# Second mask product of the first quad moved to GpSimd, and transposes, loads and copies moved around it

## The chip, the cores and the metric

The kernel runs on one core of a Trainium2 chip. The metric is the device time of one launch in microseconds (us), as the median of several runs. A profile is one execution of the same program with the hardware profiler on. The engines are called by the profile's names: PE is TensorE (PEld its weight loads), DVE is VectorE, ACT is ScalarE, POOL is GpSimd, and SP is the engine whose queue issues the stores. Every engine runs its own instructions in the order in which they are written, and waits for semaphores of the others.

## The reference, cut to what matters

```python
# 8 batches, 8 heads, 512 local and 32 global tokens, head size 64
k_all, v_all = concat(k_g, k_l), concat(v_g, v_l)            # along the tokens
out_g = softmax(q_g @ k_all.T / 8) @ v_all                   # global tokens see everything
s_ll  = where(abs(i - j) <= 32, q_l @ k_l.T / 8, -1e9)       # local tokens see a band ...
s_lg  = q_l @ k_g.T / 8                                      # ... and the global tokens
out_l = softmax(concat(s_lg, s_ll)) @ concat(v_g, v_l)
x   = concat(out_g, out_l), heads side by side               # 4352 tokens x 512
h   = x @ w_in                                               # 512 -> 2048
out = (h * sigmoid(1.702 * h)) @ w_out                       # 2048 -> 512
```

The inputs and the output are float32; the kernel computes in bf16 with float32 accumulation.

## The kernel before

Work goes by batches. A batch's attention is done by two quads of four heads, objects of class `Wide`, each with its transposed keys `kT`, queries `qt` and `qc` (a packed copy of some query columns), and its exponentials `E[0]` and `E[1]`. The steps of a quad are methods. `Tk` and `Tq` transpose keys and queries on DVE (32x32 blocks), `kcopy`, `qcopy` and `ext` copy columns of them and of the global tokens into place, `S(rnd)` multiplies queries and keys for one of two rounds, `X(rnd)` takes exp on ACT (PSUM to SBUF), `M(rnd)` multiplies the result by a 0/1 mask in place, with both inputs in SBUF. `U(unit)` makes the row sums (unit 0) and the two halves of the output, `Gm` the output of the global queries into the bank `og`; `UG` is all four. `R` transposes and inverts the row sums, `XL(h)` normalizes an output half into `xL`, the input of the hidden product. `G` normalizes the global queries' output from `og` in PSUM: reciprocal, product, transpose into `xG`.

The two products of the feed-forward part are partly written with seven products instead of eight. `Pair` (second product, two per batch) and `HPair` (a part of the hidden product) have `mm(k)` for the seven, and `m3`, `z`, `zm`, `sub`, `evict`, `add` for the sums of their results, on DVE but for the ACT copies `m3` and `evict`. In an `HPair`, `mm(5)`, `mm(2)` and `mm(7)` accumulate onto PSUM halves that `m3`, `z` and `zm` have read before. `x_sums` makes four sums of halves of `xL` that `HPair` multiplies: three of 128x512 (L673) and a fourth of 128x1024 (L674), bf16, both inputs in SBUF; `mm(3)` and `mm(4)` read the second and third, `mm(6)` the fourth. `g_sums` does the same for the activations `gT` and `Pair`.

The steady part alternates two stages, with the order of each engine written out by hand:

- `h_some(i)`, i from 3 to 7, is the hidden product of batch i with its activations, and prepares the two quads that come next: `c`, the second quad of batch i+1, and `a2`, the first of batch i+2.
- `phase_o(i)`, i from 2 to 6, is the second product of batch i (`p0`, `p1`), interleaved with attention: `a` finishes (`UG`, `R`, `XL`, `G`), `c` goes from `S` to `G`, and `a2` goes through `S`, `X`, `M` of both rounds.

PSUM has four banks for products (`pbank`, in rotation) and two pairs of banks for scores (`spair`). In the next `h_some` the hidden matmuls of step 4 take the bank `px` of `p1`, once `sub` and `evict` have read it, and those of step 5 take `py`, once `add` has. `evict` is written before the ACT table load for the activation (`gelu_table`), `m3` of the `HPair` behind it.

POOL issues the loads: `load` brings the q and k of a batch (its buffers are used by every other batch), `load_v` the v of a batch in five chunks, each with the global rows behind it but for chunk 2. `vtiles` has two buffers, so batch i+3 takes the one of batch i+1. In `phase_o(i)` POOL does `a2.M(0)` and behind it `loads_after(i + 1)`, which is `load_v(i + 3)` and `load(i + 4)` as far as there are such batches: v in `phase_o` 2, 3 and 4, q and k in 2 and 3. In `h_some(i)` POOL does the copies of `c` and `a2`.

Of the kernel before, what the change touches and what calls it, by code (L numbers as in the profile page):

```python
# [12 lines left out]
F32 = mybir.dt.float32  # L13
BF16 = mybir.dt.bfloat16
# [6 lines left out]
def kernel(  # L21
# [12 lines left out]
    nc = tc.nc  # L34

    B, H, Sl, D = q_l.shape
# [23 lines left out]
    att = ctx.enter_context(tc.tile_pool(name="att", bufs=2))  # L60
# [14 lines left out]
    def load(b, us=(0, 1), kq=True):  # L75
        if b not in loaded:
            loaded[b] = (ld.tile([128, 2, 16 * D], BF16, name="rk"),
                         ld.tile([128, 2, 16 * D], BF16, name="rq"))
        if kq:
            s = slice(us[0], us[-1] + 1)  # L80
            nc.gpsimd.dma_start(out=loaded[b][1][:, s], in_=qf[b][:, s])
            nc.gpsimd.dma_start(out=loaded[b][0][:, s], in_=kf[b][:, s])
# [5 lines left out]
    def v_view(b, n):  # L88
        return vtiles[b % 2][:, : 8 * n * (D + 2)].rearrange("p (u j c d) -> p u j c d", u=2, j=4, c=n)

    def load_v(b, hs=slice(0, 8)):
        if b == 2:
            nc.gpsimd.memset(v_view(b, 5)[:, :, :, :, D:], 1.0)
        vt = v_view(b, 5).rearrange("p u j c d -> p (u j) c d")
        vs, vg = (x[b].rearrange("h s d -> s h d") for x in (v_l, v_g))
        for c in range(5):
            n = 128 if c == 2 else 96
            nc.gpsimd.dma_start(out=vt[0:n, hs, c, :D], in_=vs[FIRST[c] : FIRST[c] + n, hs])  # L98
            if c != 2 and b != 1:
                nc.gpsimd.dma_start(out=vt[96:128, :, c, :D], in_=vg)  # L100
# [11 lines left out]
    def on_act(out_, in_):  # L112
        nc.scalar.activation(out_, in_, AF.Copy)  # L113
# [11 lines left out]
    def load_g(lo, hi, names="kq"):  # L125
        for name, dst, src in (("k", rkg, kgf), ("q", rqg, qgf)):
            if name in names:
                nc.gpsimd.dma_start(out=dst[:, lo:hi, :], in_=src[:, lo:hi, :])
# [111 lines left out]
    def transpose_g(lo, hi, names="qk"):  # L240
        for name, dst, s in (("q", qgT, rqg), ("k", kgT, rkg)):
            if name not in names:
                continue
            nc.vector.transpose(dst[:, lo:hi, :32], s[:, lo:hi].bitcast(F32))
# [31 lines left out]
    xG_by_row = xG.rearrange("p k (a s f) -> p k a s f", a=2, f=4)  # L276
# [7 lines left out]
    def spair():  # L284
        return [psS.tile([128, 2, 512], F32, name="s4", tag="s%d" % i) for i in range(2)]
# [214 lines left out]
    class Wide(Quad):  # L500
# [100 lines left out]
        def UG(self):  # L601
            for unit in range(3):
                self.U(unit)
            self.Gm()

    gTs, ops = {}, {}
    HT = TB // 2
    HM = d_model // 2
# [26 lines left out]
    def exp_table():  # L635
        nc.scalar.activation(spot[:, 0:1], spot[:, 1:2], AF.Exp)
# [27 lines left out]
    def x_sums(i):  # L664
        t = xL[i]
        x11, x12, x21, x22 = (t[:, 2 * k : 2 * k + 2, h * HT : h * HT + HT] for k in range(2) for h in range(2))
        r1 = att.tile([128, 16, 32], F32, name="sT", bufs=1).rearrange("p a b -> p (a b)").bitcast(BF16)
        r2 = att.tile([128, 512], F32, name="rs", bufs=1).bitcast(BF16)
        xs["d"] = [r.rearrange("p (k t) -> p k t", k=2) for r in (
            r1[:, : 2 * HT], r1[:, 2 * HT :], moe.tile([128, 2 * HT], BF16, name="xs"))]  # L670
        xs["s"] = r2.rearrange("p (k t) -> p k t", k=NKC)
        for o, x, y, op in zip(xs["d"], (x11, x12, x21), (x22, x22, x11), (ALU.add, ALU.subtract, ALU.subtract)):
            nc.vector.tensor_tensor(o, x, y, op)  # L673
        nc.vector.tensor_tensor(xs["s"], t[:, :, :HT], t[:, :, HT:], ALU.add)  # L674
        xs["r"] = (x11, x22)
# [173 lines left out]
    a, c = Quad(0), Quad(1)  # L849
# [93 lines left out]
    a, c = nq[1]  # L943
# [71 lines left out]
    a, c = nq[2]  # L1015
# [22 lines left out]
    def loads_after(i):  # L1038
        if i + 2 < B:
            load_v(i + 2)  # L1040
        if i == 1:
            load_g(8, NQ)
        if i + 3 < B:
            load(i + 3)

    def quads_of(n):
        if n < B and n not in nq:
            nq[n] = (Wide(2 * n), Wide(2 * n + 1))
        return nq.get(n, (None, None))
# [44 lines left out]
    def phase_o(i):  # L1094
        b = i + 1
        a, c = nq[b]
        a2, c2 = quads_of(b + 1)
        p0, p1 = Pair(i, 0), Pair(i, 1)
        exp_table()
        a.UG()  # L1100
        c.S(0)
        a.R()
        g_sums(i, 7, 8, (0,))
        a.XL(0)
        g_sums(i, 7, 8, (1, 2))
        a.XL(1)
        g_sums(i, 7, 8, (3,))
        p0.mm(3, 4, 1)
        c.X(0)
        p0.m3()  # L1110
        p0.z()
        a.G()
        c.M(0)
        c.S(1)
        c.X(1)
        p0.mm(6)
        p0.zm()
        c.M(1)
        p0.mm(5, 2)
        p0.sub()  # L1120
        p0.evict()
        p0.mm(7)
        p0.add()
        p0.store()
        if a2:
            c.UG()
            c.R()
            a2.S(0)
            a2.X(0)
            a2.M(0, nc.gpsimd)  # L1130
            loads_after(i + 1)
        else:
            pt = spair()
            c.U(0, bank(pt, 0))
            c.U(1, bank(pt, 2))
            c.U(2, bank(pt, 3))
            c.Gm(bank(pt, 1))
            c.R()
        c.XL(0)
        if a2:  # L1140
            c.XL(1)
            c.G()
        p1.mm(3, 4)
        p1.m3()
        p1.z()
        if not a2:
            c.XL(1)
            c.G()
        p1.mm(1, 6)
        p1.zm()  # L1150
        x_sums(i + 1)
        if a2:
            a2.S(1)
            a2.X(1)
        p1.mm(5, 2)
        p1.sub()
        p1.evict()
        gelu_table()
        p1.mm(7)
        p1.add()  # L1160
        if a2:
            a2.M(1)
        p1.store()

    def h_some(i):
        c = nq[i + 1][1] if i + 1 < B else None
        a2 = quads_of(i + 2)[0] if i + 2 < B else None
        pool = nc.gpsimd.tensor_copy
        gTs[i] = moe.tile([128, FC, TB], BF16, name="gT")
        hps = [pbank("hp"), pbank("hp")]  # L1170
        for fc in range(2):
            h_mm(i, fc, hps[fc], range(NKC))
        p = HPair(i, 1)
        p.mm(3, 4)
        p.m3()
        for fc in range(2):
            h_act(i, fc, hps[fc])
        if c:
            c.Tk(False)
            c.kcopy(pool)  # L1180
        p.z()
        p.mm(1, 6)
        p.zm()
        if c:
            c.Tq(False)
            c.qcopy(pool)
            c.ext((3,), pool)
        if a2:
            a2.Tk(False)
            a2.kcopy(pool)  # L1190
        h_step(i, 4)
        if c:
            c.ext((0,), on_act)
        h_step(i, 5)
        p.mm(5, 2)
        p.sub()
        p.inner()
        p.mm(7)
        p.add()
        h_step(i, 6)  # L1200
        p.outer()
        if a2:
            a2.Tq(False)
            transpose_g(2 * i + 4, 2 * i + 6)
            a2.qcopy(pool)
            a2.ext(copy=pool)
        if c:
            g_sums(i, 0, 2)
        h_step(i, 7)
        if c:  # L1210
            c.ext((1,), on_act)
            g_sums(i, 2, 4)
            for fc in range(8, 12):
                h_step(i, fc)
                if fc == 9:
                    c.ext((2,), on_act)
            g_sums(i, 4, 6)
            h_step(i, 12)
            h_step(i, 13)
            g_sums(i, 6, 7)  # L1220
            h_step(i, 14)
            h_step(i, 15)
            return
        p = HPair(i, 4)
        p.mm(3, 4)
        p.m3()
        g_sums(i, 0, 2, (0, 1))
        p.z()
        p.mm(1, 6)
        p.zm()  # L1230
        g_sums(i, 0, 2, (2,))
        h_step(i, 10)
        h_step(i, 11)
        p.mm(5, 2)
        p.sub()
        p.inner()
        p.mm(7)
        p.add()
        g_sums(i, 0, 2, (3,))
        h_step(i, 12)  # L1240
        p.outer()
        for k in range(3):
            for lo in (2, 4):
                g_sums(i, lo, lo + 2, (k,))
        h_step(i, 13)
        h_step(i, 14)
        h_step(i, 15)
        g_sums(i, 6, 8, (0, 1, 2))
        g_sums(i, 2, 4, (3,))
        g_sums(i, 4, 6, (3,))  # L1250
        g_sums(i, 6, 8, (3,))

    for i in range(1, B):
        if i > 2:
            h_some(i)
        elif i > 1:
            for fc in range(FC):
# [3 lines left out]
                if i + 1 < B:  # L1261
                    c = nq[i + 1][1]
# [6 lines left out]
                    if fc == 9 and i + 2 < B:  # L1269
                        a2 = quads_of(i + 2)[0]  # L1270
# [19 lines left out]
    for st in range(FC):  # L1290
        h_step(B, st)
        if st < len(todo):
            tt, k = todo[st]
            if k == 3:
                p = Pair(B - 1, tt, pair_banks(tt))
# [19 lines left out]
    p = Pair(B, 0, (x0, x1, y0, y1))  # L1315
# [53 lines left out]
```

## Time and profile before

| | |
|---|---|
| time, median of 3 runs | 285.33 us (285.22 to 285.46) |
| the profiled execution | 285.7 us, its span 284.0 us |
| PE busy | 277.0 us (98%), granted clock 1.0 |
| DVE, ACT, POOL busy | 228.9 us (81%), 182.1 us (64%), 107.1 us (38%) |
| mask product on POOL, 128x1760 | 4 times, 3.32 us each |
| mask product on DVE, 128x1760 and 128x1712 | 24 times, 1.05 us each |

The span runs from the first to the last instruction of the profile. Busy times are of one execution, and a busy PE need not be at its peak. A row of the timeline has its start and length in us, then engine, line, operation, what it writes and reads, its shape, how many instructions are merged in it, and in brackets the idle time before it and what ended that. DVE and ACT start an instruction some 0.1 us before the one ahead has ended, so the pitch between starts is less than the length of one.

### The profile page before, as it was taken

To read this page: it belongs to the slowest core of one execution; us is meant where nothing else is said; L and a number is where in the kernel's file an instruction comes from. 1 tells how busy PE (TensorE), PEld (TensorE's weight loads), DVE (VectorE), ACT (ScalarE), POOL (GpSimd) and SP (SyncE) were. 2 spreads that over 40 slices of the span, in tenths; PEclk is the share of its full clock that TensorE was granted. 3 is DMA by queue.
4 is the path that set the end of the run, shared out by engine and by line. 5 is a ranking of instruction groups with operands and counts; after the bars stand their busy time and mean duration, and the time that the engine had idled before them with its cause. 6 is when DMAs were issued, how large, how long until landed. Compare 5 with 4: busy or idle time off the path is not lost.

```text
span 284.0 us, 9001 instructions
## 1 busy us (share of the span) xinstructions
PE 277.0 (98%) x3763; PEld 182.3 (64%) x3763; DVE 228.9 (81%) x518; ACT 182.1 (64%) x299; POOL 107.1 (38%) x172
## 2 busy tenths in 40 slices
PE   7899999999999999999999999999999999999994
PEld 6454445544554488746885588647875589558884
DVE  7584458986689899999989998999988898586452
ACT  4858757577778784688457873788459761873331
POOL 8993550765946001990079302960041000000001
PEclk9999999999999999999999999999999999999999
DMA  7999995899999801795039802980022003200223
GB/s 208 159 195 210 203 162 77 148 217 144 170 165 183 151 2 48 78 177 91 14 69 163 150 5 68 84 97 3 21 58 74 2 3 76 74 3 0 58 54 112
DMA packets 59352, 28.24 MB, mean 99 GB/s; under 512 B 47472, under 2 KB 49776, under 8 KB 59312
## 3 DMA queue, kind: packets, MB, share of 16 engines
q0 software_dynamic: 51760, 17.83, 56.2%
q1 hardware_dynamic: 7120, 9.18, 11.7%
q8 instruction: 29, 0.48, 0.7%
q10 hardware_dynamic: 432, 0.66, 0.7%
q14 instruction: 11, 0.09, 0.1%
HBM read 36.31 MB, written 8.91 MB: 159 GB/s over the span
## 4 chain that ended last, share of the span: by engine, by line
PE 86%; DVE 7%; DMA 2%; issue 1%; POOL 1%; ACT 1%; DVEq 0%; POOLq 0%; ACTq 0%
PE hp L617 31%; PE px L800 12%; PE op L731 10%; PE py L800 9%; PE x L800 6%; PE s L560 5%; PE ov L586 5%; PE s L699 3%; PE s L617 3%; DMA rq<-in_q_l_dram 2%; DVE gs L773 2%; DVE gs L770 1%; DVE xL L471 1%; DVE kT L512 1%; PE og L597 1%
## 5 line engine op out<-in xcount | busy, mean ns | idle before, releaser
L617 PE MATMUL hp<-xL,w_in_sb 128*128 128x512 bf16 x432 | 97.0, 379 | 0.2 <-DVE xL L471 0.2
L617 PEld LDWEIGHTS <-w_in_sb 128*128 128x128 bf16 x528 | 51.4, 98 | 51.8 <-issue 0.4
L622 ACT ACTIVATE gT<-hp 128x512 bf16<-128x512 f32 x108 | 62.7, 600 | 17.1 <-PE hp L617 16.6
L571 ACT ACTIVATE e<-s 128x1016 bf16<-128x1016 f32 (+1 forms) x56 | 53.3, 1003 | 25.7 <-PE s L560 25.7
L800 PEld LDWEIGHTS <-gs 128*128 128x128 bf16 x480 | 46.2, 98 | 6.6
L576 POOL TENSOR_TENSOR e<-e,mask 128x1760 bf16<-128x1760 bf16 x4 | 13.3, 3320 | 70.0 <-ACT e L571 70.0
L98 POOL DMA_DIRECT2D v<-in_v_l_dram x40 | 31.1, 780 | 13.6 <-PE og L597 3.8
L773 DVE TENSOR_TENSOR gs<-gT 128x512 bf16<-128x512 bf16 (+1 forms) x87 | 31.6, 398 | 3.3 <-ACT gT L622 3.3
L800 PE MATMUL py<-wsum,gs 128*128 128x256 bf16 x240 | 30.3, 273 | 0.0
L731 PE MATMUL op<-w_out_sb,gT 128*128 128x512 bf16 x128 | 29.5, 380 | 0.0
L576 DVE TENSOR_TENSOR e<-e,mask 128x1712 bf16<-128x1712 bf16 (+1 forms) x24 | 25.2, 1049 | 3.5 <-ACT e L571 3.5
L512 DVE STREAM_TRANSPOSE kT<-rk 128x512 f32<-128x512 f32 x14 | 14.5, 1037 | 12.6 <-DMA rk<-in_k_l_dram 12.6
L833 POOL DMA_DIRECT2D out_dram<-ob x2 | 1.2, 596 | 60.5 <-ACT ob L113 60.3
L731 PEld LDWEIGHTS <-gT 128*128 128x128 bf16 x128 | 11.8, 98 | 14.0
L800 PEld LDWEIGHTS <-gT 128*128 128x128 bf16 x192 | 18.0, 98 | 3.0
L800 PE MATMUL px<-w_out_sb,gT 128*128 128x256 bf16 x160 | 19.2, 273 | 0.1
L800 PE MATMUL px<-w_out_sb,gs 128*128 128x256 bf16 x160 | 19.1, 273 | 0.0
L471 DVE TENSOR_TENSOR xL<-ov,rs 128x512 bf16<-128x512 f32 x27 | 17.9, 686 | 1.0 <-PE ov L438 0.3
L113 ACT ACTIVATE ob<-px 128x512 f32<-128x512 f32 x10 | 6.0, 599 | 19.3 <-DVE zz L822 19.3
L770 DVE TENSOR_TENSOR gs<-gT 128x1024 bf16<-128x1024 bf16 (+1 forms) x29 | 17.2, 598 | 0.0
L560 PEld LDWEIGHTS <-kT 32*128 32x128 bf16 x672 | 12.5, 93 | 6.8 <-issue 5.7
L100 POOL DMA_DIRECT2D v<-in_v_g_dram x24 | 14.0, 585 | 2.2 <-DMA rq<-in_q_l_dram 1.7
(176 smaller groups left out, 429.3 us busy)
## 6 DMA issues: line engine op xcount, KB each, us to landing
out_dram<-ob SPq DMA_DIRECT2D x128, 64.0 KB, 2.7
rq<-in_q_l_dram POOLq DMA_DIRECT2D x5, 512.0 KB, 8.2
rk<-in_k_l_dram POOLq DMA_DIRECT2D x5, 512.0 KB, 10.0
v<-in_v_l_dram POOLq DMA_DIRECT2D x24, 96.0 KB, 4.8
w_in_sb<-in_moe_w_in_dram POOLq DMA_DIRECT2D x8, 256.0 KB, 6.9
w_out_sb<-in_moe_w_out_dram POOLq DMA_DIRECT2D x4, 512.0 KB, 10.1
rk<-in_k_l_dram POOLq DMA_DIRECT2D x5, 256.0 KB, 7.8
rq<-in_q_l_dram POOLq DMA_DIRECT2D x5, 256.0 KB, 7.2
```

The lines of the kernel that those rows point to most:

```text
L98: nc.gpsimd.dma_start(out=vt[0:n, hs, c, :D], in_=vs[FIRST[c] : FIRST[c] + n, hs])
L471: nc.vector.tensor_mul(self.x[:, 2 * self.u + h, :], self.st[1 + h], self.st["rs"])
L512: nc.vector.transpose(flat[:, 0:Sl].rearrange("p (r t) -> p t r", t=16), loaded[self.b][0][:, self.u].bitcast(F32))
L560: nc.tensor.matmul(bank(self.ps, j)[:, at : at + n], lhsT=self.k[p, KEYS[c] : KEYS[c] + 128, e], rhs=qs[p, :, :, e], start=(e == 0), stop= ...
L571: nc.scalar.activation(self.E[rnd][:, 2 * i : 2 * i + 2, :n], self.ps[i][:, :, :n], AF.Exp, scale=scale)
L576: eng.tensor_mul(e, e, mask[:, rnd : rnd + 1, :n].to_broadcast([128, 4, n]))
L617: nc.tensor.matmul(hp[:, : width(i)], lhsT=w_in_c[:, fc // 4, kc, fc % 4 // 2, :, fc % 2], rhs=(xL[i] if i < B else xG)[:, kc, :], start=( ...
L622: nc.scalar.activation(out_, in_, AF.Gelu_apprx_sigmoid)
L731: nc.tensor.matmul(op, lhsT=gTs[i][:, fc, tci * 128 : tci * 128 + 128], rhs=w_out_sb[:, fc, :], start=(first and fc == 4 * f4), stop=(fc = ...
L770: nc.vector.tensor_tensor(sums[i][2][:, g, :n], t[:, g, 0, :n], t[:, g, 1, :n], ALU.add)
L773: nc.vector.tensor_tensor(sums[i][k][:, g, : n // 2], x[:, g], y[:, g], op)
L800: nc.tensor.matmul(out_, lhsT=lv[:, g, tt * 128 : tt * 128 + 128], rhs=rv[:, g, :], start=(g == 0 and k in ((1, 3, 4, 6) if self.apart els ...
```

## The change

In `phase_o`, for all i from 2 to 6: `G` of the two quads is replaced by `keep_og`, an ACT copy of `og` into the SBUF tile `ogs`, at the old places, and one `GG` for both quads where `c.G` stood, whose product has both inputs in SBUF. For i from 2 to 5: `Tk` and `Tq` of `c2` (the second quad of batch i+2) come from the next `h_some` to places between `p1.z`, `p1.zm` and `x_sums`; `a2.M(1)` is done by POOL in place of DVE. `load_v(i + 3)` is issued in two parts, chunks 0 and 1 ahead of `a2`'s steps and the others behind `a2.M(0)`. For i from 3 to 5: `kcopy`, `qcopy` and `ext` of `a2` come from POOL in `h_some(i)` to ACT in `phase_o(i)`.

In `h_some`: `load(i + 3)` is issued here, for i of 3 and 4; `a2.Tk` stands ahead of `z`, `a2.Tq` and `transpose_g` behind `zm`.

The order of PE's instructions is the same.

```diff
-    def load_v(b, hs=slice(0, 8)):
+    def load_v(b, hs=slice(0, 8), chunks=range(5)):
...
-        for c in range(5):
+        for c in chunks:
...
+    def keep_og(q, ogs):
+        on_act(ogs[:, q.u], q.st["og"][:, : D + 2])
+
+    def GG(b, ogs):
+        rg = att.tile([128, 2, 1], F32, name="rgg")
+        nc.vector.reciprocal(rg, ogs[:, :, D : D + 1])
+        xg = att.tile([128, 2, D], BF16, name="xgg")
+        nc.vector.tensor_mul(xg, ogs[:, :, :D], rg.to_broadcast([128, 2, D]))
+        for u in range(2):
+            nc.vector.transpose(xG_by_row[:, 2 * u : 2 * u + 2, b // 4, :, b % 4],
+                                xg[:, u].rearrange("p (d h) -> p h d", h=2))
...
 def phase_o(i):
...
+        ogs = att.tile([128, 2, D + 2], F32, name="ogs", bufs=1)
+        late = a2 and i > 2
...
         p0.z()
-        a.G()
+        keep_og(a, ogs)
+        if late:
+            a2.kcopy(on_act)
+            a2.qcopy(on_act)
         c.M(0)
...
         c.M(1)
+        if late:
+            a2.ext(copy=on_act)
...
         if a2:
             c.UG()
             c.R()
+            keep_og(c, ogs)
+            if i + 3 < B:
+                load_v(i + 3, chunks=(0, 1))
             a2.S(0)
             a2.X(0)
             a2.M(0, nc.gpsimd)
-            loads_after(i + 1)
+            if i + 3 < B:
+                load_v(i + 3, chunks=(2, 3, 4))
         else:
...
             c.R()
+            keep_og(c, ogs)
         c.XL(0)
         if a2:
             c.XL(1)
-            c.G()
+            GG(b, ogs)
         p1.mm(3, 4)
         p1.m3()
         p1.z()
-        if not a2:
+        if c2:
+            c2.Tk(False)
+        else:
             c.XL(1)
-            c.G()
+            GG(b, ogs)
         p1.mm(1, 6)
         p1.zm()
+        if c2:
+            c2.Tq(False)
         x_sums(i + 1)
...
         if a2:
-            a2.M(1)
+            a2.M(1, nc.gpsimd)
         p1.store()

 def h_some(i):
...
         if c:
-            c.Tk(False)
+            if i + 3 < B:
+                load(i + 3)
             c.kcopy(pool)
-        p.z()
-        p.mm(1, 6)
-        p.zm()
-        if c:
-            c.Tq(False)
             c.qcopy(pool)
             c.ext((3,), pool)
         if a2:
             a2.Tk(False)
-            a2.kcopy(pool)
+        p.z()
+        p.mm(1, 6)
+        p.zm()
+        if a2:
+            a2.Tq(False)
+            transpose_g(2 * i + 4, 2 * i + 6)
...
         p.outer()
-        if a2:
-            a2.Tq(False)
-            transpose_g(2 * i + 4, 2 * i + 6)
-            a2.qcopy(pool)
-            a2.ext(copy=pool)
```

## The prediction

> **What bounds the kernel now.** I read the page's busy times first, then the waits of PE, the chain of waits, and then the timeline of the steady stages engine by engine. I write o(i) for a call of `phase_o(i)` and h(i) for `h_some(i)`; the second product of batch i and the hidden product of batch i.
>
> ```profile
> PE 277.0 (98%) x3763; PEld 182.3 (64%) x3763; DVE 228.9 (81%) x518; ACT 182.1 (64%) x299; POOL 107.1 (38%) x172
> ```
>
> PE is the bound, and the waits view finds only one wait of PE behind the first 15 us, 0.2 us long. In the chain of waits, the first `U` matmul of o(2), o(3), o(5) and o(6) gives the period (start, length, in us):
>
> ```profile
> 99.74 1.20 PE ov L586 x54
> ...
> 131.05 1.20 PE ov L586 x56
> ...
> 193.97 1.20 PE ov L586 x59
> ...
> 225.28 1.20 PE ov L586 x57
> ```
>
> 131.05 - 99.74 and 225.28 - 193.97 are both 31.31. The two periods between, 193.97 - 131.05 = 62.92, are 0.30 longer than twice that. In o(4) VectorE (DVE) comes 0.1 to 0.4 late with the transpose of `R`, and the first `px` matmul waits for the bank. So 0.30 us is all that can be won: matmuls are not touched. Any wait put into PE's row comes out at the end in full, since PE has no idle time up to the tail.
>
> Now the timeline of o(5) (start, length):
>
> ```profile
> 206.75 0.28 DVE L478 TENSOR_SCALAR xg<-og,rg 128x64 bf16<-128x64 f32 x1
> 206.88 3.32 POOL L576 TENSOR_TENSOR e<-e,mask 128x1760 bf16<-128x1760 bf16 x1 [16.23 <-ACT e L571]
> ...
> 208.97 1.89 ACT L571 ACTIVATE e<-s 128x992 bf16<-128x992 f32 x2 [1.90 <-PE s L560]
> ...
> 210.74 0.41 DVE L673 TENSOR_TENSOR xs<-xL 128x512 bf16<-128x512 bf16 x1
> 211.07 0.68 DVE L674 TENSOR_TENSOR rs<-xL 128x1024 bf16<-128x1024 bf16 x1
> ...
> 211.68 0.67 DVE L822 TENSOR_TENSOR zz<-zz,px 128x512 f32<-128x512 f32 x1
> 212.44 0.60 ACT L113 ACTIVATE ob<-px 128x512 f32<-128x512 f32 x1 [1.58 <-DVE zz L822]
> ```
>
> and of DVE alone in a narrower window:
>
> ```profile
> 208.41 0.42 DVE L815 TENSOR_TENSOR zz<-zz,py 128x256 f32<-128x256 f32 x1 [0.77 <-PE py L800]
> 208.75 1.73 DVE L673 TENSOR_TENSOR sT<-xL 128x512 bf16<-128x512 bf16 x1
> ```
>
> The first sum of `x_sums` takes 1.73 where its equal at 210.74 takes 0.41. It ends at 210.48, 0.28 behind the mask product on POOL (206.88 + 3.32 = 210.20). So a DVE operation with both inputs in SBUF stands still while POOL multiplies. The add at 208.41, with one input in PSUM, took its usual 0.42 beside the same product. Smaller operations show who goes first when both want to run:
>
> ```profile
> 125.77 0.57 POOL L538 COPY q<-qgT 128x128 bf16<-128x128 bf16 x1
> ```
>
> ```profile
> 157.10 0.28 POOL L538 COPY q<-qgT 128x128 bf16<-128x128 bf16 x1
> ```
>
> The first copy came while a `g_sums` operation was running, waited some 0.29 for its end, and then ran before the next `g_sums` of DVE's full queue (issued 126.11, 0.52 long instead of 0.41). The two engines take turns.
>
> **The change part by part.**
>
> *G split.* Each `G` (0.16 + 0.28 + 0.32, a pitch of 0.68) leaves DVE; in its place are ten `keep_og` on ACT and five `GG`. An ACT copy of 128x72 takes 0.29, one of 128x256 from PSUM 0.39, so I estimate 0.25. One falls into the idle 1.03 to 1.14 before `X(1)`, the other into the 1.38 to 1.43 before the next `X(0)`: nothing on the path. `GG` is a `G` with one transpose more, about 0.85.
>
> *Copies to ACT (o(3) to o(5)).* `kcopy` of 192 and `qcopy` of 384 elements, by the line through 128x256 (0.39) and 128x512 (0.60), take 0.34 and 0.49. With `keep_og` that is 1.08 end to end, and some 0.8 in pitch (a 0.33 copy is followed 0.20 later), against the idle of 1.03 or more: zero. Without that cover `X(1)`, `M(1)`, `sub` and `evict` would move together, and `U(2)`, only some 0.1 behind `evict`, would wait 0.1 in each of three stages. The four `ext` copies (0.33, 0.33, 0.29, about 0.39) lie in the idle 1.7 before `evict`.
>
> *Loads.* Four v issues (0.82 + 0.58 + 0.77 + 0.58 = 2.75) now stand on POOL ahead of `M(0)` and wait for the last `og` matmul (141.31 in o(3)). `M(0)` then starts near 144.1, not 143.99; its reader is a whole stage away. `load` of q and k moves into h(3) and h(4), 1.42 on POOL, read 31 us later; such loads land in 8 to 10.
>
> *Tk, Tq of c2.* Pitch 0.91 + 0.63, now ahead of `x_sums`, which stood still there anyway. Transposes are not held (0.70 at 155.75 beside POOL copies). In o(2) to o(4) `x_sums` still starts before `M(0)` is over and ends within 0.2 of its old time. What is late next, `evict`, has 1.06 in hand: it ended at 213.04, and the matmul into its bank came at 214.10.
>
> *M(1) to POOL.* DVE gets back 1.05 in four stages. With the transposes gone from h(4), `g_sums` starts about 0.6 earlier, and the 0.30 of o(4) goes: **-0.30**. On POOL the product takes 1712/1760 of 3.32 = 3.23. In o(2) to o(4) it queues behind five v issues (3.6): 150.9 to 154.2 in o(3)'s time, where h(4)'s DVE work has an input in PSUM or is a transpose, and `g_sums` comes 7.3 into h. Cost zero. Behind it wait the load issues and `c`'s copies, needed some 10 us later.
>
> The Trainium skill, "GPSIMD Engine Reference", section 4.1, holds POOL to be about 2 times slower than DVE for operations with two inputs. The rows here have 3.32 against 1.06, 3.1 times; by the page's ratio the product would hold some 1.1 less and the time would be about 286.8. I take the row.
>
> *In o(5) there is no load left.* POOL is free when `M(0)` ends, near 210.3, and `M(1)` can go as soon as `X(1)` is done: 208.97 + 1.89 + 0.08 = 210.94. DVE by then: `GG` from 206.55, its product ahead of `M(0)` (206.75 against 206.88), the `z` at 207.4, `Tk`, `zm` 208.7, `Tq`, first sum held from 209.6 to 210.3, ending 210.57; then 210.50, 210.83, and the fourth sum (L674) at 211.17. `M(1)` asks at 210.94, during the third, and has its turn at 211.15: the fourth sum stands still to 214.38 and ends 0.55 later, 214.93. What hangs on that, in h(6):
>
> ```profile
> 213.88 0.38 PE L699 MATMUL s<-rs,early 128*128 128x256 bf16 x2
> ...
> 214.10 1.89 PE L617 MATMUL hp<-xL,w_in_sb 128*128 128x512 bf16 x8
> ...
> 214.46 0.37 ACT L113 ACTIVATE ob<-s 128x256 f32<-128x256 f32 x1
> ...
> 214.92 0.40 DVE L707 TENSOR_TENSOR ob<-ob,s 128x256 f32<-128x256 f32 x1
> ...
> 215.43 0.42 DVE L710 TENSOR_TENSOR ob<-ob,s 128x256 f32<-128x256 f32 x1
> 215.83 0.60 PE L699 MATMUL s<-xL,early 128*128 128x256 bf16 x4
> 216.26 0.38 PE L699 MATMUL s<-rs,early 128*128 128x256 bf16 x2
> 216.48 0.81 PE L617 MATMUL hp<-xL,w_in_sb 128*128 128x512 bf16 x3
> ```
>
> `sub` moves from 211.68 to 214.85, `evict` ends at 216.22, and the matmuls of 214.10 start at 216.28 and last to 218.01. ACT's table load and copy follow `evict` at the old distances: 217.64 to 218.01; then `z` to 218.50, `zm` to 219.03, and the last product from 219.09 to 219.31, against 216.48 before: **+2.83**. Behind it nothing is tight (DVE waits 0.88 and 0.36 there for ACT).
>
> Sum: 285.7 of the profiled execution - 0.30 + 2.83 = 288.23; the median of the runs is 0.37 below that execution, so 287.9. Bounds of the price: 2.2 if `z` and `zm` keep up with PE, 3.3 if `GG` is caught too (below).
>
> The Trainium skill, "SBUF — State Buffer", section "Who interferes with whom", speaks against this change: a DVE instruction with two SBUF inputs and a GpSimd one that reads SBUF shut each other out, the first issued keeping the ports to its end. By it the order of 210.94 and 211.17 decides as well; the 1.73 row agrees with it.
>
> **The rivals.**
>
> *The fourth sum goes first, or `M(1)` comes after it.* It has to be issued before 210.94, 0.23 earlier than I have it (0.13 by the row of before). Then POOL waits and nothing is lost: 285.33 - 0.30 = 285.0, not slower, and no change that can be told. For it: the margin is small. Against: ACT and DVE times there repeat from stage to stage within some 0.02.
>
> *`GG`'s product loses to `M(0)`.* Both its inputs now lie in SBUF (before, one was in PSUM). It leads by 0.13 in o(5), and by 0.25 and more where loads precede `M(0)`. If its reciprocal took the 0.25 of the 128x16 one rather than 0.16, 0.04 would be left. Lost in o(5), DVE stands 3.3 earlier and the first sum comes at 213.1, under `M(1)`: `sub` 0.6 to 0.8 later still, 288.6. Lost in the other three as well, each costs 2 to 5: 294 or more.
>
> *Better than the rows allow.* Faster by over 0.2%, 0.57 us (about what a measurement of this kernel can tell from no change), needs more than the 0.30 that PE waits.
>
> **How the numbers follow.** Fourth sum held: 0.71, own range 287.2 to 288.5. `GG` caught: 0.09. Nothing held: 0.17, with 0.02 of it for small ACT waits. Better: 0.03. Faster 0.03, within 0.2% 0.17, slower 0.80. The range reaches from 284.9, to take in the second case, to 288.8.
>
> **What would show it.** In o(5) the L674 sum should last near 3.8 instead of 0.68 and end 0.55 behind the second POOL product; PE should show some 2.2 us idle ahead of h(6)'s third hidden matmul group, then pieces of 0.1 to 0.5; o(2) to o(4) should take 31.31 each. I am wrong if the fourth sum runs at its usual 0.68, if a `GG` product lasts over 3 us, or if PE waits in other stages.

## The result and the profile after

| | before | after |
|---|---|---|
| median | 285.37 us (6 runs, 285.12 to 285.76) | 287.81 us (6 runs, 287.6 to 289.2) |
| ratio | | 1.0092, 95% interval 1.0072 to 1.0113 |
| periods from o(2) to o(6) | 31.31, 31.34, 31.58, 31.31 | 31.30, 31.37, 31.30, 33.90 |

The change makes the kernel 2.4 us slower, and all of it is in one stage. The profiled execution of after took 289.2 us (span 287.5), the longest of its six. Its o(2) starts 1.15 us later than that of before (100.82 against 99.67), so I compare from o(2) on. From the first `U` matmul of o(2) to the last matmul on PE, before takes 180.75 us and after 183.09.

The page's busy times of after:

```profile
PE 275.8 (96%) x3740; PEld 182.1 (63%) x3763; DVE 222.9 (78%) x504; ACT 188.3 (65%) x327; POOL 113.6 (40%) x158
```

6.0 us have left DVE and 6.5 have come to POOL, yet PE's share fell. In its chain of waits, these are the first `U` matmul of o(5) and o(6):

```profile
194.86 1.20 PE ov L586 x61
228.76 1.21 PE ov L586 x58
```

228.76 - 194.86 is 33.90, which is 2.59 above the period. The waits of PE (line, what it waited for, total, times, longest) name four new ones:

```profile
PE s L560 <- ACT q L113: 1.2, 1, 1.2
...
PE hp L629 <- ACT ob L113: 0.8, 1, 0.8
PE s L711 <- DVE rs L686: 0.8, 1, 0.8
...
PE s L711 <- DVE ob L719: 0.4, 1, 0.4
```

The first ends at 38.12, in the loading part, and is as long as the 1.15 us by which o(2) starts later. The other three are in h(6). The timeline of o(5) and h(6), where L686 is the fourth sum and L576 the mask product:

```profile
207.62 0.29 DVE L613 TENSOR_TENSOR xgg<-ogs,rgg 128x128 bf16<-128x128 f32 x1
207.76 3.35 POOL L576 TENSOR_TENSOR e<-e,mask 128x1760 bf16<-128x1760 bf16 x1 [19.82 <-ACT e L571]
...
211.87 3.28 POOL L576 TENSOR_TENSOR e<-e,mask 128x1712 bf16<-128x1712 bf16 x1 [0.77 <-ACT e L571]
211.97 3.73 DVE L686 TENSOR_TENSOR rs<-xL 128x1024 bf16<-128x1024 bf16 x1
215.62 0.68 DVE L834 TENSOR_TENSOR zz<-zz,px 128x512 f32<-128x512 f32 x1
215.75 0.38 PE L711 MATMUL s<-rs,early 128*128 128x256 bf16 x2 [0.83 <-DVE rs L686]
...
216.98 1.89 PE L629 MATMUL hp<-xL,w_in_sb 128*128 128x512 bf16 x8 [0.85 <-ACT ob L113]
...
218.75 0.42 DVE L719 TENSOR_TENSOR ob<-ob,s 128x256 f32<-128x256 f32 x1 [1.66 <-DMA out_dram<-ob]
219.22 0.60 PE L711 MATMUL s<-xL,early 128*128 128x256 bf16 x4 [0.35 <-DVE ob L719]
...
219.27 0.42 DVE L722 TENSOR_TENSOR ob<-ob,s 128x256 f32<-128x256 f32 x1
219.75 0.38 PE L711 MATMUL s<-rs,early 128*128 128x256 bf16 x2
```

Read it from the top. `GG`'s product goes 0.13 ahead of `M(0)`. `X(1)` ends at 211.80, `M(1)` starts on POOL at 211.87, and the fourth sum, issued at 211.97, lasts 3.73 instead of 0.68. `mm(6)` waits for it (215.75). `sub` (L834) starts at 215.62, `evict` follows on ACT, and step 4 waits for that (216.98). Then `mm(5)` waits for the `z` at 218.75 (219.22); the bracket there names a store, but the ACT copy `m3`, which `z` needs, ended at 218.71. By the spacing of before, PE is 0.99, 1.01 and 0.51 late at the three. `mm(7)`, at 219.75, waits for `zm` (219.27 + 0.42) and is 0.10 later still.

After o(2), the fourth sum has its usual length. DVE alone in a narrow window, then POOL:

```profile
117.91 0.41 DVE L685 TENSOR_TENSOR xs<-xL 128x512 bf16<-128x512 bf16 x1
118.25 0.68 DVE L686 TENSOR_TENSOR rs<-xL 128x1024 bf16<-128x1024 bf16 x1
```

```profile
117.30 1.72 POOL L98 DMA_DIRECT2D v<-in_v_l_dram  x2
...
120.93 3.28 POOL L576 TENSOR_TENSOR e<-e,mask 128x1712 bf16<-128x1712 bf16 x1
```

Here `M(1)` starts 2.0 us after the sum is over. How near this is to going wrong came out only in the experiments: `X(1)` had ended at 117.76, so `M(1)` was ready before the third sum (117.91) and the fourth were issued. The fourth was issued at 118.247, 6 ns behind the start of the second of the two merged v issues (118.241).

### The profile page after: what moved, and what is told of

It is laid out like the page before. It is cut to its first block, busy times and chain, and to the rows that moved or that the text cites. A ratio compares the mean times of both kernels' runs of the same rounds, so it can differ in the third digit from the quotient of the medians.

```text
span 287.5 us, 8976 instructions
## 1 busy us (share of the span) xinstructions
PE 275.8 (96%) x3740; PEld 182.1 (63%) x3763; DVE 222.9 (78%) x504; ACT 188.3 (65%) x327; POOL 113.6 (40%) x158
## 4 chain that ended last, share of the span: by engine, by line
PE 77%; DMA 11%; DVE 7%; issue 2%; POOL 2%; ACT 1%; DVEq 0%; ACTq 0%; SPq 0%; POOLq 0%
PE hp L629 29%; PE px L812 11%; PE op L743 8%; PE py L812 8%; PE x L812 6%; PE s L560 5%; DMA rk<-in_k_l_dram 5%; PE ov L586 5%; DMA w_in_sb<-in_moe_w_in_dram 3%; PE s L711 3%; DMA rq<-in_q_l_dram 2%; DVE rs L686 1%; PE s L629 1%; DVE xL L471 1%; PE og L597 1%
## 5 line engine op out<-in xcount | busy, mean ns | idle before, releaser
L629 PE MATMUL hp<-xL,w_in_sb 128*128 128x512 bf16 x417 | 95.6, 379 | 1.8 <-ACT ob L113 0.8
L785 DVE TENSOR_TENSOR gs<-gT 128x512 bf16<-128x512 bf16 (+1 forms) x87 | 30.1, 379 | 5.9 <-ACT gT L634 5.8
L576 POOL TENSOR_TENSOR e<-e,mask 128x1760 bf16<-128x1760 bf16 (+1 forms) x8 | 26.4, 3305 | 20.7 <-ACT e L571 20.6
L743 PE MATMUL op<-w_out_sb,gT 128*128 128x512 bf16 x122 | 28.9, 379 | 0.5 <-issue 0.3
L576 DVE TENSOR_TENSOR e<-e,mask 128x1760 bf16<-128x1760 bf16 (+1 forms) x20 | 21.0, 1052 | 5.5 <-ACT e L571 5.5
L560 PE MATMUL s<-q,kT 32*128 32x160 bf16 (+1 forms) x448 | 14.7, 246 | 1.2 <-ACT q L113 1.2
```

The lines of the kernel that those rows point to most:

```text
L560: nc.tensor.matmul(bank(self.ps, j)[:, at : at + n], lhsT=self.k[p, KEYS[c] : KEYS[c] + 128, e], rhs=qs[p, :, :, e], start=(e == 0), stop= ...
L576: eng.tensor_mul(e, e, mask[:, rnd : rnd + 1, :n].to_broadcast([128, 4, n]))
L629: nc.tensor.matmul(hp[:, : width(i)], lhsT=w_in_c[:, fc // 4, kc, fc % 4 // 2, :, fc % 2], rhs=(xL[i] if i < B else xG)[:, kc, :], start=( ...
L743: nc.tensor.matmul(op, lhsT=gTs[i][:, fc, tci * 128 : tci * 128 + 128], rhs=w_out_sb[:, fc, :], start=(first and fc == 4 * f4), stop=(fc = ...
L785: nc.vector.tensor_tensor(sums[i][k][:, g, : n // 2], x[:, g], y[:, g], op)
```

## The experiments

The theory: PE loses 2.6 us only because in o(5) the fourth sum stands still under POOL's `M(1)`; o(2) to o(4) cost nothing, since the v issues keep `M(1)` away. The rivals: another part of the change (`GG`, the earlier transposes, the ACT copies) holds h(6), or any `M(1)` on POOL costs something. Edits are against after where nothing else is said; "before" stands for runs of the kernel before on the same chip.

### e1: M(1) of o(5) back on DVE

```diff
-            a2.M(1, nc.gpsimd)
+            a2.M(1, nc.gpsimd if i + 3 < B else nc.vector)
```

> The changed kernel with M(1) of o(5) alone on DVE again; o(2) to o(4) keep it on POOL. Theory (the fourth sum of x_sums in o(5) is held by M(1) on POOL): the hold of 3 us and PE's waits in h(6) (0.99 + 1.01 + 0.52 us in the trace of after) go, so 287.8 - 2.6 = 285.2, or 285.05 if the 0.30 of o(4) is won in full; o(5) to o(6) takes 31.3 again. Rival (c2's transposes ahead of x_sums are what makes o(5) late): they are still there, so the time stays above 287.

285.30 us (11 runs, 285.08 to 285.83), ratio to before 1.0006, interval 0.9997 to 1.0014. The whole loss is gone with this one product. From o(2) to the last matmul it takes 180.67, against 180.75 before: 0.28 is won in o(4), and 0.19 given back in h(6). There POOL, free of `M(1)`, does its copies for h(6) from 209.56 on, beside the last three sums of o(5):

```profile
209.82 0.56 DVE L685 TENSOR_TENSOR sT<-xL 128x512 bf16<-128x512 bf16 x1
...
210.30 0.72 DVE L685 TENSOR_TENSOR xs<-xL 128x512 bf16<-128x512 bf16 x1
210.69 0.59 POOL L545 COPY kT<-kgT 128x256 bf16<-128x256 bf16 x1
210.94 0.88 DVE L686 TENSOR_TENSOR rs<-xL 128x1024 bf16<-128x1024 bf16 x1
...
214.87 0.42 DVE L719 TENSOR_TENSOR ob<-ob,s 128x256 f32<-128x256 f32 x1 [0.70 <-ACT ob L113]
```

The sums take 0.56, 0.72 and 0.88 where their usual is 0.41, 0.41 and 0.68. So `sub`, `evict` and `m3` (214.47) come later, and `mm(5)` waits for the `z` behind `m3`. `M(1)` on DVE is not what holds it: DVE stands idle for 0.70 before that `z`.

### e2: M(1) of o(5) on POOL, but behind the fourth sum

`behind` has POOL copy two elements of the fourth sum first, so that what follows on POOL waits for it.

```diff
+            if i + 3 >= B:
+                behind(xs["s"][0:1, 0, 0:2])
             a2.M(1, nc.gpsimd)
```

> The changed kernel, M(1) of o(5) still on POOL, but behind a copy of two elements on POOL that waits for the fourth sum. Theory (what costs is the moment, not that POOL does it): the product runs beside sub, add and the h(6) sums, which have an input in PSUM, and PE waits nowhere: 285.1, the same as with DVE doing it, within 0.2. Rival (POOL's 3.3 us product slows whatever DVE does, or M(1) comes too late for its reader): 286 to 288.

285.26 us (12 runs, 284.82 to 286.93), ratio 1.0008, interval 0.9996 to 1.002. The timeline of o(5):

```profile
211.35 0.68 DVE L686 TENSOR_TENSOR rs<-xL 128x1024 bf16<-128x1024 bf16 x1
...
212.24 3.23 POOL L576 TENSOR_TENSOR e<-e,mask 128x1712 bf16<-128x1712 bf16 x1
```

`X(1)` ended at 211.17; the same product on the same engine, later by one microsecond, holds nothing. So it is the order of the two, not the engine. From o(2) to the last matmul it takes 180.55, 0.20 below before, which can't be told in the median, since the start of o(2) moves by up to 1.5 us from one profile to the next (99.35 in e1, 100.82 in after). The period of o(5) is 31.30 here: POOL's copies come behind `M(1)`, and nothing is given back in h(6).

### e3 and e8: M(1) on DVE in all stages

```diff
-            a2.M(1, nc.gpsimd)
+            a2.M(1)
```

> The changed kernel with M(1) on DVE in all four stages: G split, loads, transposes and copies moved, and nothing else. Theory: in o(2) to o(4) the product on POOL hides in full and what the rest buys is the 0.30 of o(4), so this takes 285.05 to 285.2, the same as with o(5) alone put back. Rival (freeing DVE of 1.05 us in each stage matters): slower than that kernel by 0.3 or more, because g_sums come late again.

285.65 us (12 runs, 285.31 to 286.94), ratio 1.0021, interval 1.001 to 1.0033: 0.45 more than I expected at the most. The steady part is that of e1 (180.68). Behind the last matmul the profile is 0.4 us longer, and it shows 12 packets of instructions in queue 14 where the runs made with it have 11. To see whether the code's length did it, e8 is e3 with four small writes by POOL early in the kernel:

```diff
+    for _ in range(4):
+        nc.gpsimd.memset(spot_p, 0.0)
```

> The kernel with all M(1) on DVE, and four memsets of one partition and two elements more at the start of POOL's program. That kernel took 285.65 where its steady part in the profile is as short as that of the kernel with only o(5) put back (180.7 us from o(2) to the last matmul in both), and ends 0.4 later behind PE's last matmul, with one instruction fetch more in the trace (12 in queue 14, 11 in all others). Theory (that fetch at the end costs the 0.35, and where it falls goes by the length of POOL's program): 285.3 and 11 fetches. Rival (M(1) on DVE costs it): 285.65 again.

286.27 us (9 runs, 285.56 to 287.9), ratio 1.0036, interval 1.0019 to 1.0053: missed. The packets are 11 again and the end is as short as elsewhere (3.57 us behind the last matmul, in e3 3.95), but its loading part is longer (o(2) starts at 100.89, in e3 at 99.36), with the steady part at 180.6. The theory of the fetch does not hold: e10 and e11, made later, show 12 packets too and end 3.57 behind the last matmul, and the one more in e3 is of 80 bytes and lies 0.2 us behind the start of the span, not at its end. What makes e3's end longer is open. A version that is faster came from neither.

### e4: M(1) ahead of the loads in o(2) to o(4)

```diff
-            if i + 3 < B:
-                load_v(i + 3, chunks=(2, 3, 4))
...
             a2.M(1, nc.gpsimd)
+            if i + 3 < B:
+                load_v(i + 3, chunks=(2, 3, 4))
```

> The changed kernel with M(1) of o(2) to o(4) put ahead of the load of chunks 2 to 4 on POOL, so that it is ready as soon as X(1) is done, as in o(5). Theory (in those stages only the 3.6 us of load issues keep M(1) off the fourth sum): each of the three stages now pays what o(5) pays, 2.5: 287.8 + 7.5 = 295.3, with the fourth sum near 3.7 us in all four. Rival (o(5) is special, for instance by its lack of the first quad's preparation in h(6)): 288 to 290.

296.48 us (296.41 to 297.35), ratio 1.04, interval 1.0385 to 1.0414. Now o(2) does what o(5) did:

```profile
116.60 3.52 POOL L576 TENSOR_TENSOR e<-e,mask 128x1712 bf16<-128x1712 bf16 x1 [0.54 <-ACT e L571]
116.95 3.72 DVE L686 TENSOR_TENSOR rs<-xL 128x1024 bf16<-128x1024 bf16 x1
```

Each of the three stages takes 2.84 more; 3 x 2.84 = 8.5, against 296.48 - 287.81 = 8.67 measured. The loads are what kept these stages whole.

### e5: the kernel before, with nothing but M(1) on POOL

> The kernel before with one edit: M(1) of o(2) to o(5) on POOL, all else at its old place. Theory: in o(5) it is ready at 210.94 and the fourth sum is issued at 211.07, so it is held and h(6) pays some 2.5 here too; and in o(2) to o(4) the product now stands behind all loads of its stage (6 to 8 us), so that it and the copies behind it fall on the g_sums of h(3) and h(4), which come 1.5 late each: 285.3 + 2.5 + 3 = 291, between 288 and 292.5. Rival (the hold in o(5) comes only from the transposes put ahead of x_sums): o(5) pays nothing, 285.3 to 288.

296.42 us (296.01 to 297.01), ratio 1.0386, interval 1.0368 to 1.0404. h(6) pays 2.6 here too, with the old transposes, copies and `G`, so no other part of the change is needed for it. But o(3) to o(5) cost 4.1, 2.7 and 1.1 more, where I had expected some 3 in all and 292.5 at the most. There, all of a batch's loads stand ahead of `M(1)`, and it falls into the next `g_sums`:

```profile
123.63 3.26 POOL L576 TENSOR_TENSOR e<-e,mask 128x1712 bf16<-128x1712 bf16 x1
125.02 2.64 DVE L773 TENSOR_TENSOR gs<-gT 128x512 bf16<-128x512 bf16 x2
```

Two sums of some 0.4 each take 2.64, and the next, at 127.59, takes 1.62 beside POOL's copies, which `M(1)` has pushed back. The transpose of `R` comes late, and PE waits 2.56 for a bank in o(3) (6.4 in three stages). So the new places of the loads and copies are what makes `M(1)` on POOL bearable in o(2) to o(4).

### e6: GG's product behind M(0)

M(1) of o(5) as in e1, and in o(2) to o(5):

```diff
         if c2:
             c2.Tk(False)
+            GG(b, ogs)
```

in place of `GG` ahead of `p1.mm(3, 4)`.

> The changed kernel with M(1) of o(5) on DVE, and GG behind c2's key transpose in o(2) to o(5), 0.9 us later, so that its product comes after M(0) has started on POOL. Theory (whichever of the two comes first keeps the other out, and the 0.13 by which the product leads M(0) is what the change lives on): the product lasts some 2.7 to 3 us, x_sums end 2 us later, and each of the four stages pays 1.6: 285.3 + 6.5 = 291.8; up to 299 if the fourth sum comes so late that M(1) of o(2) to o(4) catches it too. Rival (a product of 128 elements is too short to be held, or DVE catches up): 285.3 to 286.

309.69 us (308.52 to 310.6), ratio 1.0836, interval 1.0809 to 1.0864, where I had expected 299 at the most. `GG`'s product is held for 2.95 as the rival of the prediction had it, but then something that none of the theories had:

```profile
113.25 2.95 DVE L613 TENSOR_TENSOR xgg<-ogs,rgg 128x128 bf16<-128x128 f32 x1
...
118.01 5.14 DVE L685 TENSOR_TENSOR sT<-xL 128x512 bf16<-128x512 bf16 x1
...
119.60 3.25 POOL L576 TENSOR_TENSOR e<-e,mask 128x1712 bf16<-128x1712 bf16 x1
```

The first sum was issued 1.6 us before `M(1)` started, and yet stood until `M(1)` was over; POOL was issuing loads in between. The "turns" of the prediction do not give this. e9 to e11 are about it.

### e7: sub ahead of the fourth sum in o(5)

```diff
-        x_sums(i + 1)
+        x_sums(i + 1, i != 5)   # all but the fourth sum
...
         p1.sub()
+        if i == 5:
+            x_sum4(i + 1)       # the fourth sum
```

> The changed kernel, in o(5) with sub ahead of the fourth sum, which is held by M(1) as before. Theory (of the 2.5 of after, 1.0 is mm(6) waiting for the sum and 1.5 is evict and what follows it on ACT, late because sub stands behind the sum): 287.8 - 1.5 = 286.3. Rival (all of it hangs on the sum itself, or on DVE being 3 us behind): 287.5 to 287.8.

286.19 us (8 runs, 285.94 to 286.46), ratio 1.0027, interval 1.0017 to 1.0037: as expected. The fourth sum is held as before (3.12), but `sub` and `evict` no longer stand behind it, `z` and `zm` come in time, and only `mm(6)`'s wait of 0.99 is left.

### e9 and e10: one more v issue moved ahead of M(0)

In both, M(1) of o(5) as in e1, and chunk 2, which is a single issue, moved ahead:

```diff
-                load_v(i + 3, chunks=(0, 1))
+                load_v(i + 3, chunks=(0, 1, 2))
...
-                load_v(i + 3, chunks=(2, 3, 4))
+                load_v(i + 3, chunks=(3, 4))
```

In e10, `M(1)` of o(2) to o(4) also stands behind `behind(xs["s"][0:1, 0, 0:2])`, as in e2. Theory A: a product that is ready and near enough in POOL's queue holds DVE already while POOL issues loads. B: only a product that runs does.

> The kernel with M(1) of o(5) on DVE, and of the v load three chunks ahead of M(0) and two behind it, where there were two and three. In the run with GG late, a first sum issued at 118.01 stood still to 123.15, although M(1) started only at 119.60 and POOL had nothing but load issues until then; M(1) had been ready since 116.5 and was the third in POOL's queue. Here the fourth sum is issued about 0.1 behind M(0)'s release of the sums, near 119.0, with M(1) started near 121 and again third in the queue. Theory A (an operation of POOL that is ready and only a few places from its turn keeps DVE out already): the fourth sum ends at 124.7, each of o(2) to o(4) pays 4 to 6.5, 297 to 305. Theory B (only a running one does; the long wait there had another cause): M(0) and the sums end 0.8 later, evict still has 0.2 in hand, 285.3 to 286.

> The same split of the load, and M(1) of o(2) to o(4) on POOL behind a copy of two elements that waits for the fourth sum, so that it is not ready while the sums run. Theory A: nothing keeps DVE out, 285.3 to 286. Theory B gives the same; it is the control: if this one is slow too, the split of the load itself costs, and the run before it tells nothing.

e9: 308.57 us (306.49 to 310.11), ratio 1.0803, interval 1.0722 to 1.0884. e10: 287.26 us (287.25 to 287.79), ratio 1.0069, interval 1.0048 to 1.009. The timeline of e9 in o(2), where the first row is two sums merged:

```profile
115.36 8.02 DVE L685 TENSOR_TENSOR sT<-xL 128x512 bf16<-128x512 bf16 x2
...
119.84 3.25 POOL L576 TENSOR_TENSOR e<-e,mask 128x1712 bf16<-128x1712 bf16 x1
```

`M(0)` ended at 117.17 and let the first sum go; the second was issued at 117.39 and ended at 123.38, 6 us later, of which `M(1)` ran only the last 3.3. `X(1)` had ended at 116.70. In e10, with the same loads and an `M(1)` that is not ready until the fourth sum is done, no sum is held. It has 0.68 per stage of its own, since DVE starts later there: the slack of `evict` is used up, and PE waits 0.36 in each of the three stages for the `z` behind `m3`. The difference of the two, 21 us, is the hold and what follows from it. A is borne out, by more than expected, and two sums earlier: the second one, not the fourth.

### e11: the fourth sum 0.6 us later in o(2) to o(4)

M(1) of o(5) as in e1, and the edit of e7 for i below 5 instead of 5.

> The kernel with M(1) of o(5) on DVE, and in o(2) to o(4) sub ahead of the fourth sum, which so is issued some 0.6 later. In the trace of after the fourth sum of o(2) to o(4) is issued 0.006 to 0.019 behind the start of the second load issue that follows M(0) (118.247 against 118.241 in o(2)), with three more issues and then M(1) behind that one, and runs at its usual 0.68. Theory A (M(1), once ready, keeps DVE out from some place in POOL's queue on, about three issues ahead of its turn): 0.6 later the sum is held, to the end of M(1), 5 us later, mm(6) waits some 3.7 in each of three stages: 296; M(1) was off the fourth sum in o(2) to o(4) by much less than the 2 us between the sum's end and M(1)'s start. Theory B (only a running product does): nothing hangs on 0.6 there, 285.3 to 285.8.

302.7 us (301.96 to 303.32), ratio 1.0596, interval 1.0549 to 1.0644: A again, though 6.7 us above the 296 expected. DVE in o(2), then POOL:

```profile
118.17 5.89 DVE L678 TENSOR_TENSOR rs<-xL 128x1024 bf16<-128x1024 bf16 x1
```

```profile
117.57 0.77 POOL L98 DMA_DIRECT2D v<-in_v_l_dram  x1
...
120.26 3.24 POOL L576 TENSOR_TENSOR e<-e,mask 128x1712 bf16<-128x1712 bf16 x1
```

The sum was issued 0.60 into the second v issue, 2.1 ahead of `M(1)`, and ended 0.56 behind it. In after the same sum, issued 6 to 19 ns into the same issue, ran in 0.68. The periods of o(3) and o(4) are 5.7 longer than after's 31.3, of which PE waits 4.0 for `mm(6)`; the rest is in the windows (us; busy time and count of PE, PEld, DVE, ACT, POOL; granted clock; DMA share; GB/s):

```profile
124.10:127.00 2.90, 2.89 (x9) 1.22 (x9) 2.79 (x6) 0.56 (x2) 1.96 (x5) 0.54 0.57 97
127.00:130.00 3.00, 3.00 (x19) 1.64 (x18) 1.65 (x5) 2.12 (x6) 0.00 (x0) 1.00 1.13 203
```

PE came back at half clock: 9 matmuls in 2.9 us, then 19 in 3.0. The low step lasts 3.41 us and costs about half of that, 5.7 - 4.0 = 1.7.

## Why the prediction was right, point by point

**The mechanism and its place.** Right. The fourth sum of o(5) stood still under `M(1)`, and ended 0.55 behind it (215.70 against 215.15), as forecast. e1 and e2 take away that meeting alone and get the whole loss back; e4 makes it three times more and pays three times more.

**The order that decided.** `M(1)` had to come before the fourth sum's issue, forecast with 0.23 in hand (0.13 by the row of before); it came with 0.10. The sign was right by a narrower margin than the text had it, but e9 and e11 show that the margin was of another kind: `M(1)` was ready from 211.80 on with nothing ahead of it in POOL's queue, and in those runs readiness, not the start, is what held DVE. Counted so, it came with 0.17.

**+2.83.** Mis-sized: +2.59. The waits for `mm(6)` and `evict` measured 0.99 and 1.01; the sum gave 1.12 and 1.06 (215.0 against 213.88, and 216.28 less that delay against 214.10). Behind `evict` it is 0.61 (0.51 for `z`, 0.10 for `zm`), where the sum gave 0.65 (2.83 less 2.18). So the order of the steps was right to the end, and the largest error is in the first: `M(1)` did not wait for the end of the third sum, as the working had it. It started 0.08 behind the end of `X(1)`, at 211.87, while the third sum, issued at 211.64, lasted to 212.05. 2.59 lies inside the bounds of 2.2 and 3.3.

**-0.30.** Measured -0.28 in o(4). It is real and is the only gain. A later o(3) (31.37 against 31.34) gives back 0.03.

**The zeros.** The periods 31.30, 31.37 and 31.30 bear out that the copies on ACT, `GG`, the loads and the transposes cost nothing where they were put, but for the 0.03. -0.28 + 2.59 + 0.03 = 2.34, the difference of 183.09 and 180.75.

**`GG`'s product.** It led by 0.13 in o(5), as forecast, and by 0.38 in the others, and the rival that it loses did not happen. Counted by readiness, as e9 and e11 suggest, the lead was smaller: `X(0)` ended 0.05 behind the product's issue in o(5) (207.68 against 207.62), 0.05 and 0.06 behind it in o(3) and o(4), and 0.01 ahead of it in o(2) (113.64 against 113.65). No run shows how much of that could have been lost. e6 shows what it would have cost in four stages: not 2 to 5 each, as the rival said, but some 6 (309.69 - 285.3 = 24.4). PE waited 9.6 for `z` behind the held product, and 4.8 more for the first sum and 2.5 for `evict`, which come of a second hold that the prediction didn't know. Its granted clock was 0.5 for three steps of 3.41 (from 116.6, 202.0 and 232.7), some 1.7 each by the working of e11. The rest was not taken apart.

**What was right by luck.** "Cost zero" for `M(1)` in o(2) to o(4) came out, but its reason was too weak. The prediction thought of five v issues as 3.6 us of distance. What the runs show is a product that holds DVE while it has two or three issues still ahead of it (e6, e9, e11), so the distance in hand was not 2 us but less than 0.6 at the fourth sum. And "the two engines take turns" does not hold everywhere. In before, a `g_sums` operation issued at 156.71 took 1.26. DVE alone, then POOL:

```profile
156.71 1.26 DVE L773 TENSOR_TENSOR gs<-gT 128x512 bf16<-128x512 bf16 x1
```

```profile
156.65 0.50 POOL L507 COPY qc<-q 128x384 bf16<-128x384 bf16 x1
157.10 0.28 POOL L538 COPY q<-qgT 128x128 bf16<-128x128 bf16 x1
157.34 0.30 POOL L540 COPY q<-qgT 128x144 bf16<-128x144 bf16 x1
```

It was issued while the copy of 156.65 ran, and ended at 157.97; its usual length is 0.41. By turns it would have come next; the copies of 157.10 and 157.34 both ran while it stood. The prediction showed the copy of 157.10, for its length, and did not look at the sum that it passed.

The Trainium skill, "SBUF — State Buffer", section "Who interferes with whom", gives the ports to whichever of the two was issued first, for the whole instruction. The 2.95 of e6 agree with that. e9 and e11 don't, if the start in the profile is taken for the issue: there DVE's sum came 2 us and more ahead and lost. The measurement decides: in these runs a ready product in POOL's queue counted before its row started.

**What stays open.** At which place of POOL's queue the hold begins was not settled: all three held sums had two or three issues between the running one and `M(1)`, and the fourth sums that passed, with three between as well, were issued within 19 ns of an issue's start. The third sums of o(2) to o(4) in after had four between and a ready `M(1)`, and passed in 0.41. So it begins near the third issue ahead, as far as the starts of POOL's rows in the profile can be trusted. Why the hold exists was not measured either: whether POOL had begun on the product before its row starts, or it only stood in the queue, the profile does not tell. No version beats before: e1 and e2 are equal to it, because PE waits only 0.3 us in the steady part, so that VectorE's 6 us are worth nothing on the path.

## What to carry to other kernels

Before moving work to an engine that can shut out another, as POOL does DVE here, list every operation of the other engine that may be issued from the moment the moved one is *ready*, not from when it is expected to run; loads queued ahead of it are a poor fence (three were none in e9 and e11), a wait on the other engine's result is one (e2, e10). Where a stage is free only thanks to what stands beside it (here the v issues), look for the one iteration in which that is missing: the last one has no load left, and that is where the time went. And a busy engine off the path is worth relieving only by as much as the bound engine waits for it, here 0.3 us.

## What the runs showed of the hardware

- A POOL product that is ready kept a DVE operation with two inputs in SBUF out while POOL still issued the two or three DMAs ahead of it: 5.1 us in e6, 6.0 in e9, 5.9 in e11, for products of 3.25. With four DMAs ahead it did not (the sum of 117.91 in after, 0.41), and one that waits for a semaphore did not (e2, e10).
- After waits of 3.8 us and more (e9, e11), PE's granted clock was 0.5 for a step of 3.41 us, once for two. After waits of 2.0 to 2.9 us it was so only at times: in e5 behind the 2.56 us of o(3), not behind the 2.89 us of o(4). After waits of up to 1.2 us (after and e4) it stayed at 1.0. The Trainium skill, "TensorE: Matmul & The Clock Gate", section "What's actually happening", has half speed after an idle window of about 3.4 us (3413 ns); the 3.41 agrees with that length, though the 2.56 us of e5 are shorter than a whole window.
